# Routing attention and a feed-forward block on one core: a turn's products reordered by how they divide TensorE's array

## The chip, the core and the metric

One NeuronCore of a Trainium2 chip. The metric is the device time of one execution in microseconds, median of 3 runs. The engines are TensorE (PE, matrix products), VectorE (DVE), ScalarE (ACT), GpSimd (POOL) and SyncE (SP, which issues the DMAs here). Each engine takes its instructions in its own order, and waits on semaphores for the others.

TensorE's array has 128 x 128 cells. A product whose weights have fewer rows or columns than 128 uses a part of it, and two such products can stand in the array side by side. "How a product divides the array" means that choice: 128 x 128 (one product), 64 x 128 (two, by rows), 128 x 64 (two, by columns), 128 x 32 (four, by columns).

## The reference

Attention in which a query sees only the keys that are assigned to the same centroid, and then a feed-forward block with a quick GELU over the joined heads.

```
batch, n_heads, seq, head_dim = (4, 8, 768, 64)     # 16 clusters
q_assign = argmax(einsum('bhsd,hcd->bhsc', q_n, c_n))   # q_n, k_n, c_n: normalised
k_assign = argmax(einsum('bhsd,hcd->bhsc', k_n, c_n))
mask = q_assign[:, :, :, None] == k_assign[:, :, None, :]
scores = scale * matmul(q, k.transpose(0, 1, 3, 2))
scores = where(mask, scores, -1e9)
attn = exp(scores - max(scores)); attn /= sum(attn) + 1e-9
x = matmul(attn, v)  ->  (batch * seq, n_heads * head_dim) = (3072, 512)
h = x @ w_in                                         # 512 x 2048
g = h * (1 / (1 + exp(-1.702 * h)))
out = g @ w_out                                      # 2048 x 512
```

q, k, v and the centroids are fp32; the two weight matrices come in 8-byte floats and are turned into fp32 on the chip.

## The kernel before

`fast` does the work; `general`, a slower way for inputs outside a limit, is skipped here by a branch on a value that `fast` computes (`is_bad`).

**Units and turns.** Two heads make a pair, 16 pairs in all (`p`), each with its 768 positions on the free axis. A group is one pair and one half of its queries (384), and has six units, one per 128 keys. The main loop (L546) goes over turns `t`; a turn takes two units. Three turns make a group, 24 turns a batch (`TB`), 96 turns the whole, and two more end the pipeline. The first batch is special: its pairs (`p < HP`) are masked by adding a product on TensorE (`part`, L398) ahead of the exponential; the other pairs are masked afterwards, on DVE (`mask`, L420).

**What a turn does**, in the order in which it is written, which is the order of each engine's queue:

1. `scores` (L384): keys times queries of two heads, 64 x 128, into the PSUM pool `ps_s`, two buffers.
2. `part` (L398), first batch only.
3. `exps` (L409) on ACT.
4. `round_next`: one step of turning weights into fp32 (L159 to L177 on DVE, ACT and POOL), 33 steps in all; from turn 12 on there is a second one late in the turn.
5. `mask` (L420), four DVE instructions that read the exponentials in PSUM, and the running sum of the units on POOL (L430).
6. Half of the turn's feed-forward chunks.
7. `prep`, the preparation of a later pair, one step or more: `prep_turn` (four steps, transposes of q and k, L262, and their copy on ACT, L267), `prep_near` (centroid products L276, 128 x 32, and a copy L282), `prep_assign` (transposes L287, then argmax on DVE, L293 to L316), and `prep_hot` (first batch: L349, L354, L356) or `prep_spread` (L323, the copy L328 of a row of codes, and two DMAs, L330 and L332). Step 0 and steps 1 and 3 also issue the loads of v (L120), q and k (L111).
8. `values` of the turn before (L441): 128 x 64, into `ps_o`; after a group's last unit the copy L446.
9. Every third turn (t = 4, 7, 10, ...) `normalise` of a group: the sums over keys (L453, 128 x 64, with a matrix of ones), a reciprocal (L456) and a product (L458) on DVE, and on ACT two passes that accumulate the sums and the reciprocals for the branch's test (L462).
10. The other half of the feed-forward chunks.

**Feed-forward chunks.** When the four groups of half a batch are normalised, 28 chunks are put in the queue `ffn`: 16 of `first` (L480: four 128 x 128 products of 384 columns with w_in, tanh L485 on ACT, product L487 on DVE) and 12 of `second` (L497: four products of 512 columns with w_out; each fourth one ends with a copy L503 and a store L504). `rate` is 28 per 11.5 turns; `owed` carries the fraction.

**PSUM banks.** Transposes, centroid products, L323, L349, the sums of `normalise`, `first` and `second` all take their bank from the pool `ps_m`, whose three buffers are called `m`. A buffer is given again when its last reader is done, and a TensorE instruction that writes it waits for that reader. An accumulation of `second` holds its buffer for four chunks.

**The end.** After the loop DVE reduces the sums' test to one number by way of a transpose (L578 to L587); `values_load` (L589) makes every engine wait for it, and the chunks that are left, one half batch less one, follow.

Of the kernel before, what the change touches and what calls it, by code (L numbers as in the profile page):

```python
# [18 lines left out]
def kernel(  # L19
    tc: tile.TileContext,  # L20
    q: bass.AP,
    k: bass.AP,
    v: bass.AP,
    centroids: bass.AP,
    moe_w_in: bass.AP,
    moe_w_out: bass.AP,
    out: bass.AP,
):

    args = (q, k, v, centroids, moe_w_in, moe_w_out, out)
    bad = fast(tc, *args)
    with tc.If(bad > 0):
        general(tc, *args)
# [3 lines left out]
def fast(  # L39
# [33 lines left out]
    NF = DF // P  # L73
# [24 lines left out]
    def bank():  # L98
        return ps_m.tile([P, 512], FP32, name="m")

    def short():
        return tmp.tile([P, HALF], FP32, name="short")
# [4 lines left out]
    def load_qk(p, w):  # L107
        t = inp.tile([P, NJ, 2, D], FP32, name="in")
        b, hp = divmod(p, HP)
        for a in range(2):  # L110
            nc.sync.dma_start(  # L111
                out=t[:, :, a, :],
                in_=(q, k)[w][b, 2 * hp + a].rearrange("(p j) d -> p j d",
                                                       j=NJ))
        qk_in[p, w] = t

    def load_v(p):
        b, hp = divmod(p, HP)
        t = pairs.tile([P, 2, NJ, D], FP32, name="inv")
        nc.sync.dma_start(  # L120
            out=t.rearrange("p a j d -> p a (j d)"),
            in_=v[b, 2 * hp:2 * hp + 2].rearrange(
                "a (p j) d -> p a (j d)", j=NJ))
        v_in[p] = t
# [57 lines left out]
    def round_next():  # L182
        i = w_done[0]
        if i < NW:
            load_w(i + 2)
            split_w(i)
        if 0 < i <= NW:
            join_w(i - 1)
        w_done[0] += 1
# [66 lines left out]
    def prep_turn(p, i):  # L256
        w, h = divmod(i, 2)
        if h == 0:
            T[p, w] = pairs.tile([P, S], FP32, name=f"T{w}")
        ps = bank()  # L260
        for n in range(NH):
            nc.tensor.transpose(out=ps[:, n * P:(n + 1) * P],  # L262
                                in_=qk_in[p, w][:, h * NH + n].rearrange(
                                    "p a d -> p (a d)"),
                                identity=ident)
        dst = T[p, w][:, h * HALF:(h + 1) * HALF]
        nc.scalar.copy(dst, ps[:, 0:HALF])  # L267
# [95 lines left out]
    PREP = [lambda p, i=i: prep_turn(p, i) for i in range(4)]  # L363
# [9 lines left out]
    def split(g):  # L373
        b, r = divmod(g, 2 * HP)
        h, hp = divmod(r, HP)
        return b * HP + hp, h

    def scores(u):
        g, kt = divmod(u, NJ)
        p, h = split(g)  # L380
        ps = ps_s.tile([P, 2, 512], FP32, name="s")
        for a in range(2):
            rows = slice(a * D, (a + 1) * D)
            nc.tensor.matmul(out=ps[:, a, 0:HALF],  # L384
                             lhsT=T[p, 1][rows, kt * P:(kt + 1) * P],
                             rhs=T[p, 0][rows, h * HALF:(h + 1) * HALF],
                             start=True, stop=(p >= HP))
        s_of[u] = ps[:, :, 0:HALF]

    def part(u):  # L390

        g, kt = divmod(u, NJ)
        p, h = split(g)
        if p >= HP:
            return
        for a in range(2):
            r = 32 * (2 * (p % 2) + a)
            nc.tensor.matmul(  # L398
                out=s_of[u][:, a, :],
                lhsT=hots[p // 2, 1][r:r + NC, kt * P:(kt + 1) * P],  # L400
                rhs=hots[p // 2, 0][r:r + NC, h * HALF:(h + 1) * HALF],
                start=False, stop=True)

    def exps(u):
        p, h = split(u // NJ)
        s = s_of[u]
        if p < HP:
            A_of[u] = ap.tile([P, 2, HALF], FP32, name="A")
        nc.scalar.activation(out=A_of[u] if p < HP else s, in_=s, func=AF.Exp,  # L409
                             scale=SCALE)  # L410

    def mask(u):

        g, kt = divmod(u, NJ)
        p, h = split(g)
        s = s_of.pop(u)
        if p >= HP:
            A_of[u] = ap.tile([P, 2, HALF], FP32, name="A")
            for a in range(2):
                nc.vector.scalar_tensor_tensor(  # L420
                    out=A_of[u][:, a, :],
                    in0=qcode[p][:, a, h * HALF:(h + 1) * HALF],
                    scalar=code[p][:, kt % NH, 1, kt // NH, a:a + 1],
                    in1=s[:, a, :], op0=ALU.is_equal, op1=ALU.mult)
        A = A_of[u]
        if kt == 0:
            return
        if kt == 1:
            sum_of[g] = ap.tile([P, 2, HALF], FP32, name="sum", bufs=2)
        nc.gpsimd.tensor_tensor(out=sum_of[g],  # L430
                                in0=A_of[u - 1] if kt == 1 else sum_of[g],
                                in1=A, op=ALU.add)

    def values(u):
        g, kt = divmod(u, NJ)
        p, h = split(g)
        if kt == 0:
            o_of[g] = ps_o.tile([P, 512], FP32, name="o")
        A = A_of.pop(u)
        for a in range(2):  # L440
            nc.tensor.matmul(out=o_of[g][a * D:(a + 1) * D, 0:HALF],  # L441
                             lhsT=v_in[p][:, a, kt, :], rhs=A[:, a, :],
                             start=(kt == 0), stop=(kt == NJ - 1))
        if kt == NJ - 1:
            O_of[g] = xp.tile([P, HALF], FP32, name="x")
            nc.scalar.copy(O_of[g], o_of.pop(g)[:, 0:HALF])  # L446

    def normalise(g):

        sm = sum_of.pop(g)  # L450
        ps = bank()
        for a in range(2):
            nc.tensor.matmul(out=ps[a * D:(a + 1) * D, 0:HALF], lhsT=ones,  # L453
                             rhs=sm[:, a, :], start=True, stop=True)
        rec = short()
        nc.vector.reciprocal(out=rec, in_=ps[:, 0:HALF])  # L456
        x = xT_of[g] = O_of.pop(g)
        nc.vector.tensor_tensor(out=x, in0=x, in1=rec, op=ALU.mult)  # L458

        junk = short()  # L460
        for i, t in enumerate((ps[:, 0:HALF], rec)):
            nc.scalar.activation(out=junk, in_=t, func=AF.Copy,  # L462
                                 accum_out=sums[:, i, g:g + 1])
        if g % HP == HP - 1:
            ffn.extend(ffn_chunks(g // HP))


    ffn = deque()
# [50 lines left out]
    prep_at = {}  # L519
    for p in range(1, NPAIR):  # L520
        b, hp = divmod(p, HP)
        for i in range(2 if p == 1 else 0, len(PREP)):
            if p == 1:
                t = (i - 2) // 2
            elif b == 0:
                t = (hp - 2) * TG + 1 + i // 2
            else:
                t = b * TB + (-20, -8, -2, 1)[hp] + i
# [5 lines left out]
    def prep(p, i):  # L534
        if i == 0 and p:
            load_v(p)
        PREP[i](p)
        if i in (1, 3) and loads:
            load_qk(*loads.popleft())

    rate = (NF + NH * (NF // 4)) / (TB / 2 - 0.5)
    owed = 0.0
# [3 lines left out]
    for t in range(NT + 2):  # L546
        us = range(2 * t, 2 * t + 2) if t < NT else ()
        for u in us:
            scores(u)
        if t == 0:  # L550
            prep(0, 6)
        for u in us:
            part(u)
        for u in us:
            exps(u)
        round_next()
        for u in us:
            mask(u)
        owed = owed + rate if ffn else 0.0
        n = min(int(owed), len(ffn))  # L560
        owed -= n
        for _ in range((n + 1) // 2):
            ffn.popleft()()
        for p, i in prep_at.get(t, ()):
            prep(p, i)
        if 1 <= t <= NT:
            for u in range(2 * t - 2, 2 * t):
                values(u)
        if t >= 2 and (t - 2) % TG == TG - 1:
            normalise((t - 2) // TG)  # L570
        if t >= TB // 2:
            round_next()
        for _ in range(n // 2):
            ffn.popleft()()


    ok = const.tile([P, 2, 2 * NPAIR], FP32, name="ok")
# [1 line left out]
                            op0=ALU.is_le)  # L579
    ok1 = const.tile([P, 1], FP32, name="ok1")  # L580
    nc.vector.tensor_reduce(out=ok1, in_=ok, axis=AX.XY, op=ALU.min)
    ps = bank()
    nc.tensor.transpose(out=ps[0:1, 0:P], in_=ok1, identity=ident)
    okt = const.tile([1, 1], FP32, name="okt")
# [448 lines left out]
```

## Time and profile before

| | us |
|---|---|
| median of 3 runs (1107.4, 1107.4, 1109.77) | 1107.4 |
| the profiled execution | 1111.25 |
| its span, first to last instruction | 1109.4 |
| L480, busy (1024 records, two per product) | 359.1 |
| L497, busy (768) | 348.7 |
| L384, busy (768) | 151.9 |
| L441, busy (768) | 149.8 |
| L262, busy (192) | 32.9 |
| L456 on DVE, mean of one | 2.557 |
| L462 on ACT, mean of one, from PSUM | 0.492 |

An fp32 product shows as two records of TensorE. The record's duration reaches beyond the start of the next one, since products are pipelined; what a product costs is read from start to start. In the timeline rows of one form that follow one another are merged ("x8"), with the start of the first, the time from there to the end of the last, engine, line, operation, tiles, shapes; in brackets stands how long the engine was idle before and what ended that.

Turn starts can be read from the first L384 of each turn: turn 14 at 103.13, turn 24 (the first of the second batch) at 222.73, turn 37 at 372.73, turn 38 at 376.31, turn 40 at 393.63, turn 41 at 405.67, turn 42 at 414.49, turn 95, the last with scores, at 986.33.

### The profile page before, as it was taken

The page shows a single profiled execution, that of the slowest core. Times are in us where ns is not written, and L with a number is a line of the kernel's source. Part 1 is how long each engine was busy: PE and PEld are TensorE (multiplying, and loading weights), DVE is VectorE, ACT ScalarE, POOL GpSimd, SP SyncE. Part 2 cuts the span into 40 slices and gives each one's busy share as a digit, 9 for nine tenths or more (in the row PEclk, how much of TensorE's full clock was granted, in tenths as well). Part 3 has the DMA queues.
Part 4 walks back from the last instruction along what each step waited for, and adds up shares of the span by engine and source line. Part 5 has one row for each costly group of instructions (what it writes and reads, how often), then busy time and mean ns, then how long its engine had stood idle before and what let it go on. Part 6 is the DMA issues. An engine that isn't in the chain of part 4 may idle for free. (4 is left out here: it accounts for less than half of the span.)

```text
span 1109.4 us, 10492 instructions
## 1 busy us (share of the span) xinstructions
PE 1069.4 (96%) x3982; PEld 490.4 (44%) x3982; DVE 470.0 (42%) x711; ACT 348.3 (31%) x665; POOL 338.6 (31%) x200
## 2 busy tenths in 40 slices
PE   6786999999999999999999999999999999999997
PEld 3332454444443445444444445444544444444543
DVE  4779986134542444323543254433452244421200
ACT  4564554233322333223331233223322132211100
POOL 2577655322222333122231243223132233320000
PEclk9989899999999999999999999999999999999999
DMA  9443342110100010101100000020000000000000
GB/s 232 135 130 105 116 128 71 46 48 20 45 22 27 10 29 15 31 25 53 50 22 17 19 15 16 14 67 12 8 8 10 9 10 1 1 10 19 1 10 22
DMA packets 64812, 45.13 MB, mean 41 GB/s; under 512 B 51952, under 2 KB 57584, under 8 KB 64752
## 3 DMA queue, kind: packets, MB, share of 16 engines
q1 hardware_dynamic: 64608, 44.33, 14.2%
q8 instruction: 33, 0.54, 0.2%
q14 instruction: 27, 0.22, 0.1%
q10 hardware_dynamic: 144, 0.03, 0.0%
HBM read 38.04 MB, written 6.31 MB: 40 GB/s over the span
## 5 line engine op out<-in xcount | busy, mean ns | idle before, releaser
L480 PE MATMUL m<-x,w_in 128*128 128x384 f32 x1024 | 359.1, 499 | 6.2 <-DVE x L458 4.8
L430 POOL TENSOR_TENSOR sum<-sum,A 128x768 f32<-128x768 f32 x128 | 234.1, 1829 | 382.8 <-DVE A L420 366.6
L497 PE MATMUL m<-w_out,g 128*128 128x512 f32 x768 | 348.7, 601 | 0.0
L480 PEld LDWEIGHTS m<-x,w_in 128*128 128x128 f32 x1024 | 188.0, 191 | 171.2 <-issue 40.6
L420 DVE SCALAR_TENSOR_TENSOR A<-qb,code,s 128x384 f32<-128x384 uint8 x288 | 157.6, 610 | 250.3 <-ACT s L409 226.7
L497 PEld LDWEIGHTS m<-w_out,g 128*128 128x128 f32 x768 | 140.2, 190 | 188.8 <-issue 185.0
L487 DVE SCALAR_TENSOR_TENSOR g<-g,m 128x384 f32<-128x384 f32 x128 | 70.9, 554 | 200.5 <-ACT g L485 199.7
L384 PE MATMUL s<-T,T 64*128 64x384 f32 x768 | 151.9, 514 | 2.6 <-ACT A L409 2.6
L441 PE MATMUL o<-A,inv 128*64 128x384 f32 x768 | 149.8, 512 | 0.0
L409 ACT ACTIVATE s<-s 128x768 f32<-128x768 f32 x144 | 107.9, 791 | 94.0 <-PE s L384 93.8
L485 ACT ACTIVATE g<-m 128x384 f32<-128x384 f32 x128 | 62.4, 487 | 217.1 <-PE m L480 217.0
L456 DVE RECIPROCAL short<-m 128x384 f32<-128x384 f32 x32 | 81.8, 2557 | 103.7 <-PE m L453 103.7
L430 POOL TENSOR_TENSOR sum<-A 128x768 f32<-128x768 f32 x32 | 58.9, 1842 | 190.7 <-DVE A L420 190.5
L384 PEld LDWEIGHTS s<-T,T 64*128 64x128 f32 x768 | 66.5, 188 | 90.5 <-issue 50.0
L441 PEld LDWEIGHTS o<-A,inv 128*64 128x64 f32 x768 | 47.5, 139 | 69.7 <-issue 68.5
L462 ACT ACTIVATE short<-m 128x384 f32<-128x384 f32 x32 | 15.7, 492 | 142.9 <-DVE short L456 142.9
L503 ACT ACTIVATE y<-m 128x512 f32<-128x512 f32 x24 | 14.3, 594 | 102.4 <-PE m L497 89.0
L267 ACT COPY T<-m 128x384 f32<-128x384 f32 x64 | 29.5, 479 | 46.8 <-PE m L262 46.7
L409 ACT ACTIVATE A<-s 128x768 f32<-128x768 f32 x48 | 36.2, 809 | 23.7 <-PE s L398 23.7
L446 ACT COPY x<-o 128x384 f32<-128x384 f32 x32 | 15.4, 480 | 77.0 <-PE o L441 77.0
L177 POOL TENSOR_TENSOR w_in<-w_in,e 128x512 f32<-128x512 f32 x16 | 24.7, 1543 | 44.6 <-DVE w_in L174 42.2
L262 PE MATMUL m<-ident,in 128*128 128x128 f32 x192 | 32.9, 291 | 4.1 <-ACT qb L356 1.7
(67 smaller groups left out, 397.9 us busy)
## 6 DMA issues: line engine op xcount, KB each, us to landing
raw<-in_moe_w_in_dram SPq DMA_DIRECT2D x16, 512.0 KB, 4.6
raw<-in_moe_w_out_dram SPq DMA_DIRECT2D x16, 512.0 KB, 3.5
in<-in_q_dram SPq DMA_DIRECT2D x32, 192.0 KB, 3.7
in<-in_k_dram SPq DMA_DIRECT2D x32, 192.0 KB, 3.5
inv<-in_v_dram SPq DMA_DIRECT2D x16, 384.0 KB, 4.5
out_dram<-y SPq DMA_DIRECT2D x24, 256.0 KB, 2.0
qb<-line SPq DMA_DIRECT2D x12, 192.0 KB, 3.0
line<-row SPq DMA_DIRECT2D x12, 1.5 KB
```

What stands on the lines that cost most here:

```text
L262: nc.tensor.transpose(out=ps[:, n * P:(n + 1) * P], in_=qk_in[p, w][:, h * NH + n].rearrange("p a d -> p (a d)"), identity=ident)
L267: nc.scalar.copy(dst, ps[:, 0:HALF])
L384: nc.tensor.matmul(out=ps[:, a, 0:HALF], lhsT=T[p, 1][rows, kt * P:(kt + 1) * P], rhs=T[p, 0][rows, h * HALF:(h + 1) * HALF], start=True, ...
L409: nc.scalar.activation(out=A_of[u] if p < HP else s, in_=s, func=AF.Exp, scale=SCALE)
L420: nc.vector.scalar_tensor_tensor(out=A_of[u][:, a, :], in0=qcode[p][:, a, h * HALF:(h + 1) * HALF], scalar=code[p][:, kt % NH, 1, kt // NH ...
L430: nc.gpsimd.tensor_tensor(out=sum_of[g], in0=A_of[u - 1] if kt == 1 else sum_of[g], in1=A, op=ALU.add)
L441: nc.tensor.matmul(out=o_of[g][a * D:(a + 1) * D, 0:HALF], lhsT=v_in[p][:, a, kt, :], rhs=A[:, a, :], start=(kt == 0), stop=(kt == NJ - 1))
L456: nc.vector.reciprocal(out=rec, in_=ps[:, 0:HALF])
L480: nc.tensor.matmul(out=ps[:, 0:HALF], lhsT=w_in[:, c, f * P:(f + 1) * P], rhs=xT[c], start=(c == 0), stop=(c == NCH - 1))
L485: nc.scalar.activation(out=g, in_=ps[:, 0:HALF], func=AF.Tanh, scale=0.851)
L487: nc.vector.scalar_tensor_tensor(out=g, in0=g, scalar=1.0, in1=ps[:, 0:HALF], op0=ALU.add, op1=ALU.mult)
L497: nc.tensor.matmul(out=ps[:, 0:DM], lhsT=hs[f][:, n * P:(n + 1) * P], rhs=w_out[:, f, :], start=(f == 0), stop=(f == NF - 1))
```

## The change

The order within a turn becomes: scores, part, exponentials, `round_next`, mask; then of the preparation only the centroid products (`prep_near`); then values of the turn before; then `normalise`, where there is one; then the other steps of the preparation; then the second `round_next`; then all feed-forward chunks of the turn in one piece. `prep` is called in a different order but with the same steps in each turn, so its DMAs go along with it. The chunks are popped one at a time while `owed` is 1 or more. At the end, eight `first` chunks are issued ahead of the transpose of the branch's test. Nothing is added or left out.

```diff
         for u in us:
             mask(u)
-        owed = owed + rate if ffn else 0.0
-        n = min(int(owed), len(ffn))
-        owed -= n
-        for _ in range((n + 1) // 2):
-            ffn.popleft()()
-        for p, i in prep_at.get(t, ()):
-            prep(p, i)
+        work = sorted(prep_at.get(t, ()), key=lambda w: PREP[w[1]] != prep_near)
+        while work and PREP[work[0][1]] == prep_near:
+            prep(*work.pop(0))
         if 1 <= t <= NT:
             for u in range(2 * t - 2, 2 * t):
                 values(u)
+        owed = owed + rate if ffn else 0.0
         if t >= 2 and (t - 2) % TG == TG - 1:
             normalise((t - 2) // TG)
+        for p, i in work:
+            prep(p, i)
         if t >= TB // 2:
             round_next()
-        for _ in range(n // 2):
+        while owed >= 1 and ffn:
             ffn.popleft()()
+            owed -= 1
...
     nc.vector.tensor_reduce(out=ok1, in_=ok, axis=AX.XY, op=ALU.min)
+    for _ in range(NF // 2):
+        ffn.popleft()()
     ps = bank()
     nc.tensor.transpose(out=ps[0:1, 0:P], in_=ok1, identity=ident)
```

## The prediction

> **What bounds the kernel now.** First the page: the busy shares, the slices, the clock.
>
> ```profile
> PE 1069.4 (96%) x3982; PEld 490.4 (44%) x3982; DVE 470.0 (42%) x711; ACT 348.3 (31%) x665; POOL 338.6 (31%) x200
> ...
> PE   6786999999999999999999999999999999999997
> ...
> PEclk9989899999999999999999999999999999999999
> ```
>
> TensorE (PE) is idle for some 31 us of the first 120 (table of stretches: 18.5, 22.5, 26.7 and 21.0 busy of 30 each) and then hardly at all until the end (199.9 of 200 from 400 to 600); DVE is next at 42%. From 120 us on every ns of PE's row counts, so I read it in the timeline, here turns 40 to 42. "x8" are eight records, two per fp32 product; start to start is the price.
>
> ```profile
> 400.81 1.51 PE L441 MATMUL o<-A,inv 128*64 128x384 f32 x8
> ...
> 402.15 0.82 PE L453 MATMUL m<-sum,ones 128*64 128x384 f32 x4
> ...
> 402.89 2.85 PE L480 MATMUL m<-x,w_in 128*128 128x384 f32 x8
> ...
> 405.61 0.49 ACT L462 ACTIVATE short<-m 128x384 f32<-128x384 f32 x1 [4.16 <-DVE short L456]
> ...
> 405.67 1.56 PE L384 MATMUL s<-T,T 64*128 64x384 f32 x8
> ...
> 407.16 2.85 PE L480 MATMUL m<-x,w_in 128*128 128x384 f32 x8
> ...
> 409.85 0.49 PE L262 MATMUL m<-ident,in 128*128 128x128 f32 x3
> ...
> 410.27 1.51 PE L441 MATMUL o<-A,inv 128*64 128x384 f32 x8
> ```
>
> At the end, where L480 runs without interruption, chunks follow every 2.58 us:
>
> ```profile
> 1025.94 0.49 ACT L485 ACTIVATE g<-m 128x384 f32<-128x384 f32 x1 [2.09 <-PE m L480]
> ...
> 1028.52 0.49 ACT L485 ACTIVATE g<-m 128x384 f32<-128x384 f32 x1 [2.09 <-PE m L480]
> ```
>
> So a record takes 2.58/8 = 0.323. Between other shapes the chunk takes 405.67 - 402.89 = 2.78, 0.20 more. L384 is four pairs, 1.29, and takes 407.16 - 405.67 = 1.49, again 0.20 more. L441 takes 1.34 when L453, its own shape, follows (0.05 over 1.29), and 1.44 when L480 does (411.71 - 410.27, next row). Three transposes take 0.42 before L441, 0.33 among themselves (0.109 each). A change of shape thus costs **0.10 on leaving**, and **on entering** 0.10 for L480, L497 and L384, 0.05 for L441, 0.06 for transposes (L276 to L262 to L441: 252.37 to 252.85 is 0.48, not 0.42).
>
> **The change: what it removes.** In the order of the built program a turn with feed-forward work has four changes before (L384, block, L441, block, L384) and three after. Counted from turn 14 to the end there are 373 before and 281 after: 92 leavings, 92 x 0.10 = 9.2 us. Entries by L480 or L497 fall from 161 to 37 (124 x 0.10 = 12.4), entries by transposes rise from 13 to 45 (32 x 0.06 = 1.9), those of L384, L441 and L276 stay equal in number. **Gain 19.7, say 20 us.** Transposes directly ahead of L480 or L497, 45 times, are not in this trace: nothing if the next weights load under 0.109 as they do among transposes, 0.10 each (4.5 in all) if as badly as across a change; I take nothing, the nearer row.
>
> **What it moves: normalise, ahead of transposes and feed-forward.** Its L453 takes one of the three "m" banks. The bank comes free when L462 has read it, and L462 waits for the reciprocal L456 (4.16 above). Before, behind L453 came one feed-forward block with two banks free. Now the transposes (up to two banks), L323 (one) and the whole block come behind it, and in the built program's waits a PE instruction of 18 of those turns waits for that L462. The wait, with its price, occurs once in the early part before:
>
> ```profile
> 50.09 2.56 DVE L456 RECIPROCAL short<-m 128x384 f32<-128x384 f32 x1 [4.96 <-PE m L453]
> ...
> 52.74 0.49 ACT L462 ACTIVATE short<-m 128x384 f32<-128x384 f32 x1 [4.27 <-DVE short L456]
> ...
> 53.38 0.55 PE L262 MATMUL m<-ident,in 128*128 128x128 f32 x3 [0.61 <-ACT short L462]
> ```
>
> When is the bank free? Count from the start S of the turn's scores. The reciprocal stands behind the turn's four masks on DVE. Turn 37, which has no feed-forward, already has the new order:
>
> ```profile
> 372.73 1.56 PE L384 MATMUL s<-T,T 64*128 64x384 f32 x8
> ...
> 374.64 2.19 DVE L420 SCALAR_TENSOR_TENSOR A<-qb,code,s 128x384 f32<-128x384 uint8 x4 [11.44 <-ACT s L409]
> ...
> 376.75 2.55 DVE L456 RECIPROCAL short<-m 128x384 f32<-128x384 f32 x1
> ```
>
> The reciprocal starts at S + 4.02, L462 2.58 later (its row there is 379.33), PE goes on 0.64 after that (52.74 to 53.38): **S + 7.24**. When does PE want it? Scores 1.49, values 1.34, sums 0.74: S + 3.57. L323 takes 0.15 (343.04 to 343.19), three transposes 0.33 + 0.06, a chunk 2.58. By the order of each turn:
> - L323, then transposes without a bank (turns 46, 70): wanted at 3.72, 3.52 each, 7.0. Turn 22 has no masks (reciprocal 0.86 after L453, as 402.15 to 403.01) but 0.43 of L398: 3.2.
> - Two groups of transposes (25, 49, 73): the second at 3.96, 3.28 each, 9.8.
> - L323 and two groups (28, 52): 4.11, 3.13; then 0.5 for the copy L328, queued on ACT behind both L462 (1.23, 405.61 to 406.84) and taking 0.25; 7.3.
> - L323, transposes, chunk (31, 55, 76): 4.11, 3.13 each, 9.4.
> - One of the two, then two chunks (40, 43, 64, 67; 79; 16, 19): the second chunk at 6.54, 6.4 and 6.97: 4 x 0.70 + 0.84 + 2 x 0.38 = 4.4.
>
> **Loss 41 us**, eleven waits of over 3 us (36.7) and seven short ones. The other turns have a bank. Below bound of this term: nothing, if the bank came free by S + 3.7; above: 18 x 3.65 = 66, if every one waited in full.
>
> Queued behind L462 on ACT are now the copies of transposes (L267) and the tanh (L485), ahead of it before: used a turn later, or when their chunk ends, so free. L330 and L332 are issued some 4 us later on SP; their first reader is at least two turns (18 us) on, against 3.0 to land. The loads L111 and L120 that go along with prep on SP are read three turns on or later, against 3.7 to 4.5 to land. The sums that L453 reads, now up to 6 us sooner, are done by POOL a turn before (two L430 of 1.85 behind masks). Values come up to 6 us earlier, at S + 1.49, a whole turn after the masks that end at S + 4.1 of the turn before: free; if a turn shrank to 3.58, as turn 37, still 0.97 left.
>
> **What the waits do to the clock.** The table of stretches (PE busy of 3.41 us, then DVE, ACT, POOL, the clock):
>
> ```profile
> 36.15:39.56 3.41, 1.19 (x11) 0.65 (x9) 1.68 (x3) 2.34 (x5) 2.18 (x3) 1.00 0.31 72
> 39.56:42.98 3.42, 3.42 (x13) 1.34 (x10) 3.28 (x8) 0.48 (x1) 0.95 (x1) 0.50 0.21 81
> ...
> 56.63:60.04 3.41, 1.50 (x14) 0.34 (x12) 0.89 (x2) 3.41 (x8) 3.41 (x2) 1.00 1.04 262
> ...
> 97.59:101.00 3.41, 1.83 (x12) 0.49 (x8) 2.66 (x2) 0.72 (x1) 3.33 (x3) 1.00 0.52 163
> 101.00:104.42 3.42, 2.16 (x12) 0.80 (x12) 3.42 (x3) 2.03 (x3) 3.42 (x3) 1.00 0.00 0
> ```
>
> The clock changes on a grid of 3.41 us. Stretches with PE busy 1.50 or less (five) are followed by half speed, of 3.4, 6.8, 3.4, 6.8 and 3.4 us; those with 1.81 or more are not. A wait of 3.1 to 3.5 leaves under 1.75 busy in one stretch wherever it starts, but for about one start in ten. Half speed costs 1.7 per stretch, two stretches where the idle time runs on past the edge by 0.5 or more (about a third of the starts). I take 2.0 for each of eleven: **22 us**; ends 0 and 11 x 3.41 = 37.5.
>
> The Trainium skill, "TensorE: Matmul & The Clock Gate", section on HAM oscillation, says that only idle gaps above about 3.4 us should be avoided, a whole window. By it most of these waits would leave the clock alone and the sum would be 1124 as in the first rival; the trace shows half speed after 1.9 us of idle time in a stretch, and I go by the trace.
>
> **Before turn 14** PE waits for ACT and DVE. Values now stand where PE waited for L282 (2.95, 2.22, 2.46; 1.5 hidden each), for L308 (0.8), for L316 (2.0), for x at the first chunk (1.5 of 4.83): -8.8. In turns 4 and 7 transposes now wait for L462: 7.35 - 4.86 = 2.5 each, of which turn 4 waited 1.7 already: +3.3. DVE, 27.9 busy of 30 from 90 to 120, gives some back: **-4**, between -9 and +5. **At the end** the test waits behind the last early chunk's tanh and product on DVE instead of 0.93 for L581: 0, within 1.
>
> Sum: -20 + 41 + 22 - 4 = **+39** on the span of 1109.4, so 1148. That execution took 1111.25, 3.85 above the median of 1107.4; the difference carries over: **1146**.
>
> **The rivals.**
> - *The clock holds.* Waits as above, no half speed: 1107.4 + 17 = 1124. For it: short waits in 97 to 104 us passed. Against: five of five deep stretches did not. 0.17.
> - *Two stretches after each wait*: 1107.4 - 20 + 41 + 37 - 4 = 1161. For it: two of five. 0.10.
> - *Faster: normalise's bank isn't late.* If L462 read it without the reciprocal, or the reciprocal passed the masks, eleven waits would vanish: 1107.4 - 24 = 1083. It decides from a release before S + 5.7, where the long waits are halved and stay under the clock's 1.9. Against: L462 waits for L456 in all rows seen, and DVE keeps its order. 0.05; break-even near that point 0.02.
>
> **How the numbers follow.** 0.66 for the sum, 1146. Its own terms reach from 1134 to 1160. The range takes the clock's rival in: 1120 to 1162. A change under 0.3% (3.3 us) can't be told from none; only the last rival gets there. Faster 0.05, same 0.02, slower 0.93.
>
> **What would show it.** Among PE's waits after the change, L262, L480 and L497 for ACT L462: about 18 from turn 14 on, some 40 us, the longest 3.5; 0.5 in the clock right behind them; L441 1.49 behind L384; chunks of 2.58 from the second on. Wrong if PE stays at 99.9% from 200 to 1000 us, or if the clock keeps 1.00 through waits of 3 us.

## The result, and the profile after

| | before | after |
|---|---|---|
| median, the two run side by side (4 runs each) | 1108.45 us | 1147.78 us |
| lowest to highest | 1107.4 to 1109.77 | 1145.69 to 1150.5 |
| profiled span | 1109.4 | 1145.4 |
| mean granted TensorE clock | 0.989 | 0.976 |

The ratio is **1.0356, 95% interval 1.0329 to 1.0382**: the change makes the kernel 3.6% slower. The page of the changed kernel, busy shares, slices and clock:

```profile
PE 1066.3 (93%) x3982; PEld 500.1 (44%) x3982; DVE 486.7 (42%) x711; ACT 350.3 (31%) x665; POOL 336.3 (29%) x200
...
PE   6787799988989999898889999988989999999997
...
PEclk9899999999999999999999999999999999999999
```

TensorE does the same 3982 instructions in 3 us less busy time, but its slices, which before read 9 without a break from the fifth to the last but one, now have 8s in three groups. Each group lies at the start of a batch of 24 turns, where the turns with normalise whose preparation also wants banks stand close together (turns 22 to 31, 46 to 55, 70 to 76). What PE waited for there, from 118 us to the end (total us, times, longest):

```profile
PE m L262 <- ACT short L462: 25.3, 8, 3.4
PE m L480 <- ACT short L462: 14.4, 10, 3.0
PE m L480 <- DVE g L487: 3.1, 1, 3.1
...
PE m L480 <- ACT row L328: 0.5, 2, 0.2
```

That is 39.7 us in 18 waits for L462, the pass that reads normalise's bank; before, no PE wait of that kind was left after 118 us. One of them in full, in the timeline of turn 28 of the changed kernel:

```profile
275.17 1.56 PE L384 MATMUL s<-T,T 64*128 64x384 f32 x8
...
276.66 1.51 PE L441 MATMUL o<-A,inv 128*64 128x384 f32 x8
...
277.09 2.19 DVE L420 SCALAR_TENSOR_TENSOR A<-qb,code,s 128x384 f32<-128x384 uint8 x4 [0.74 <-ACT s L409]
...
278.00 0.82 PE L453 MATMUL m<-sum,ones 128*64 128x384 f32 x4
...
278.90 0.55 PE L262 MATMUL m<-ident,in 128*128 128x128 f32 x3
279.19 2.55 DVE L456 RECIPROCAL short<-m 128x384 f32<-128x384 f32 x1
281.78 0.49 ACT L462 ACTIVATE short<-m 128x384 f32<-128x384 f32 x1 [4.10 <-DVE short L456]
...
282.42 0.55 PE L262 MATMUL m<-ident,in 128*128 128x128 f32 x3 [2.97 <-ACT short L462]
...
283.21 7.12 PE L480 MATMUL m<-x,w_in 128*128 128x384 f32 x16 [0.25 <-ACT row L328]
```

Read it from the bottom up. PE's second group of transposes waits 2.97 for the bank of L453. ACT sat idle for 4.10 before L462, the bank's last reader: its first pass needs only the sums, but it starts at 281.78, 0.04 after the reciprocal L456 ended on DVE. L456 reads the same bank, so that the bank has two readers that come late. DVE starts the reciprocal when the turn's four masks end. The 16 records of L480 behind it span 7.12, though two chunks span 5.33 at full speed. The table of stretches says why (PE busy is the second number, the granted clock the third from the right):

```profile
276.92:280.34 3.42, 2.53 (x16) 0.97 (x12) 3.25 (x5) 0.76 (x2) 1.89 (x2) 1.00 0.00 0
280.34:283.75 3.41, 1.09 (x5) 0.72 (x6) 2.10 (x2) 1.94 (x7) 1.72 (x1) 1.00 0.00 0
283.75:287.16 3.41, 3.41 (x7) 1.79 (x6) 0.00 (x0) 0.15 (x1) 0.00 (x0) 0.50 0.21 64
...
829.88:833.30 3.42, 2.14 (x14) 0.83 (x10) 3.42 (x5) 0.37 (x1) 2.27 (x2) 1.00 0.00 0
833.30:836.71 3.41, 1.72 (x6) 1.06 (x7) 1.71 (x2) 1.71 (x6) 1.33 (x1) 1.00 0.00 0
836.71:840.12 3.41, 3.41 (x12) 1.90 (x10) 0.56 (x1) 0.49 (x1) 0.00 (x0) 1.00 0.16 58
```

After the stretch in which PE was busy for 1.09, the clock is 0.50 for one stretch: 3.41 us at half speed, 1.71 lost. The last three rows are turn 76, whose wait is as long (2.97 too) but is divided by the grid's edge into 1.28 and 1.69 of idle time: the clock stays at 1.00, and that turn is 2.84 us longer than before, where turns 31 and 55, with the same order of work, are 4.29 and 4.45 longer.

### The profile page after: what moved, and what is told of

Same layout as the page of the kernel before. It is cut to its first block, busy times and chain, and to the rows that moved or that the text cites. A ratio compares the mean times of both kernels' runs of the same rounds, so it can differ in the third digit from the quotient of the medians.

```text
span 1145.4 us, 10477 instructions
## 1 busy us (share of the span) xinstructions
PE 1066.3 (93%) x3982; PEld 500.1 (44%) x3982; DVE 486.7 (42%) x711; ACT 350.3 (31%) x665; POOL 336.3 (29%) x200
## 5 line engine op out<-in xcount | busy, mean ns | idle before, releaser
L480 PE MATMUL m<-x,w_in 128*128 128x384 f32 x1024 | 352.6, 499 | 22.3 <-ACT short L462 14.4
L497 PE MATMUL m<-w_out,g 128*128 128x512 f32 x768 | 345.8, 606 | 0.0
L480 PEld LDWEIGHTS m<-x,w_in 128*128 128x128 f32 x1024 | 193.7, 194 | 166.8 <-ACT short L462 19.4
L497 PEld LDWEIGHTS m<-w_out,g 128*128 128x128 f32 x768 | 146.8, 195 | 179.6 <-issue 177.3
L487 DVE SCALAR_TENSOR_TENSOR g<-g,m 128x384 f32<-128x384 f32 x128 | 70.4, 553 | 269.7 <-ACT g L485 269.4
L384 PE MATMUL s<-T,T 64*128 64x384 f32 x768 | 154.2, 521 | 5.4 <-ACT A L409 5.4
L441 PE MATMUL o<-A,inv 128*64 128x384 f32 x768 | 145.6, 500 | 0.0
L456 DVE RECIPROCAL short<-m 128x384 f32<-128x384 f32 x32 | 81.7, 2552 | 27.2 <-PE m L453 27.2
L441 PEld LDWEIGHTS o<-A,inv 128*64 128x64 f32 x768 | 46.8, 136 | 84.6 <-issue 84.6
L262 PE MATMUL m<-ident,in 128*128 128x128 f32 x192 | 37.2, 317 | 35.2 <-ACT short L462 32.3
L462 ACT ACTIVATE short<-m 128x384 f32<-128x384 f32 x32 | 15.7, 491 | 127.6 <-DVE short L456 127.6
L262 PEld LDWEIGHTS m<-ident,in 128*128 128x128 f32 x192 | 23.2, 155 | 55.3 <-ACT short L462 34.2
L171 DVE SCALAR_TENSOR_TENSOR e<-raw,e 128x512 int32<-128x512 int32 x32 | 33.7, 1054 | 2.7 <-ACT e L163 2.7
```

The lines of the kernel that those rows point to most:

```text
L171: nc.vector.scalar_tensor_tensor(out=e, in0=raw[:, :, 1], scalar=-2 ** 31, in1=e, op0=ALU.bitwise_and, op1=ALU.bitwise_or)
L262: nc.tensor.transpose(out=ps[:, n * P:(n + 1) * P], in_=qk_in[p, w][:, h * NH + n].rearrange("p a d -> p (a d)"), identity=ident)
L384: nc.tensor.matmul(out=ps[:, a, 0:HALF], lhsT=T[p, 1][rows, kt * P:(kt + 1) * P], rhs=T[p, 0][rows, h * HALF:(h + 1) * HALF], start=True, ...
L441: nc.tensor.matmul(out=o_of[g][a * D:(a + 1) * D, 0:HALF], lhsT=v_in[p][:, a, kt, :], rhs=A[:, a, :], start=(kt == 0), stop=(kt == NJ - 1))
L480: nc.tensor.matmul(out=ps[:, 0:HALF], lhsT=w_in[:, c, f * P:(f + 1) * P], rhs=xT[c], start=(c == 0), stop=(c == NCH - 1))
L487: nc.vector.scalar_tensor_tensor(out=g, in0=g, scalar=1.0, in1=ps[:, 0:HALF], op0=ALU.add, op1=ALU.mult)
```

## The experiments

All ratios are to the kernel before, run side by side with the experiment on the same chip. The theory: the loss comes from one bank, which normalise's L453 fills and which is held until the reciprocal and then L462 have read it, and from the half-speed clock behind the waits for it; the saving of shape changes is real and lies under it. The rivals: the new order as such costs (a longer block of chunks, values sooner), or the copies of the transposes, queued on ACT behind L462, are what is late.

**Prep alone (e5).** The kernel before, with only the preparation moved behind values and normalise; chunks stay in two pieces.

```diff
-        for p, i in prep_at.get(t, ()):
-            prep(p, i)
         if 1 <= t <= NT:
             for u in range(2 * t - 2, 2 * t):
                 values(u)
         if t >= 2 and (t - 2) % TG == TG - 1:
             normalise((t - 2) // TG)
+        for p, i in prep_at.get(t, ()):
+            prep(p, i)
```

> The kernel before, with one part of the change alone: the preparation is called behind values and normalise; feed-forward stays in two halves, 360 changes of shape instead of 373 (3.8 us less). Bank theory: eleven turns have two or three steps behind the sums that need the third bank, 2.8 to 3.3 us each, 32 us, and half speed after eight to ten of them, 14 to 17 us: 1107.4 - 4 + 32 + 15 + 2 = 1152, between 1143 and 1160. Rival (one block of feed-forward is what costs): 1104.

Measured 1142.96 us, ratio 1.0306 (1.027 to 1.0341). This one move, which saves hardly any shape changes (360 are left of 373), loses 34 us by itself. PE's waits from 130 us on:

```profile
PE m L262 <- ACT short L462: 13.7, 5, 2.8
PE m L497 <- ACT short L462: 8.0, 3, 2.7
PE m L480 <- ACT short L462: 7.9, 3, 2.6
```

They are 29.6 us in eleven. The time is 9 under the middle of what was expected, at its very edge (1143). Some 5 of that is the clock, since only six of the eleven waits are followed by half speed, where eight to ten were expected, and some 2 the waits, expected at 32; the rest wasn't traced. These waits are 2.6 to 2.8, the ones of the changed kernel 3.0 to 3.4. Four rows of the table of stretches of this run:

```profile
516.38:519.79 3.41, 1.49 (x6) 0.96 (x7) 1.80 (x2) 1.94 (x6) 0.00 (x0) 1.00 0.74 196
519.79:523.20 3.41, 3.41 (x12) 1.45 (x12) 0.00 (x0) 0.63 (x2) 0.00 (x0) 1.00 0.09 34
...
553.92:557.34 3.42, 1.38 (x6) 0.88 (x7) 1.68 (x2) 2.08 (x7) 0.00 (x0) 1.00 0.00 0
557.34:560.75 3.41, 3.41 (x7) 1.50 (x5) 0.00 (x0) 0.00 (x0) 0.00 (x0) 0.50 0.34 92
```

Busy for 1.49, and the clock holds; busy for 1.38, and it halves.

**The bank set free early (e1, e2).** The changed kernel, with L462's first pass, the one that reads PSUM, ahead of the reciprocal. It leaves a copy in SBUF, from which the reciprocal is taken: the same sums, but the bank no longer waits for DVE. The edit takes both late readers off the bank, the pass and the reciprocal; neither was moved alone.

```diff
-        rec = short()
-        nc.vector.reciprocal(out=rec, in_=ps[:, 0:HALF])
+        cp = short()
+        nc.scalar.activation(out=cp, in_=ps[:, 0:HALF], func=AF.Copy,
+                             accum_out=sums[:, 0, g:g + 1])
+        rec = short()
+        nc.vector.reciprocal(out=rec, in_=cp)
         x = xT_of[g] = O_of.pop(g)
         nc.vector.tensor_tensor(out=x, in0=x, in1=rec, op=ALU.mult)
-        junk = short()
-        for i, t in enumerate((ps[:, 0:HALF], rec)):
-            nc.scalar.activation(out=junk, in_=t, func=AF.Copy,
-                                 accum_out=sums[:, i, g:g + 1])
+        nc.scalar.activation(out=cp, in_=rec, func=AF.Copy,
+                             accum_out=sums[:, 1, g:g + 1])
```

> The changed kernel, but L462's first pass reads the sums ahead of the reciprocal and leaves a copy in SBUF, which the reciprocal reads; its second pass stays where it was. Theory (normalise's PSUM bank is late, because its reader waits for the reciprocal): the bank is free at about S + 4.3 instead of 7.25, so of the 18 waits A, B and D shrink to 0.2 to 0.6 each; the row copy L328 still stands behind the second pass, which waits for the reciprocal, so turns 28 and 52 keep 2.8 and turns 31, 55, 76 keep 0.6. Sum 11 us of waits and some 3 of clock: 1107.4 - 20 - 4 + 14 = 1097. Rival (the queue of ACT, which still holds the copies and the tanh behind a pass that waits for the reciprocal): no change against the changed kernel, 1147. Rival (feed-forward in one piece costs by itself): above 1130.

Measured 1104.11 us, ratio 0.9949 (0.9934 to 0.9964): 45 us gone from the changed kernel by an edit that leaves the order of PE's work alone. It is 7 above what was expected. The kernel before, run beside it, took 1109.71, 2.3 more than the 1107.4 of the sum; the rest wasn't traced, and it isn't in the waits, of which there are no more than foreseen. From 130 us on they are, but for 0.3 and the one at the end:

```profile
PE m L480 <- ACT row L328: 7.3, 5, 2.8
PE m L262 <- ACT short L456: 2.2, 6, 0.5
```

(L456 is the first pass here.) The second pass still waits for the reciprocal, and behind it on ACT stands the copy of the row of codes, L328, whose bank is late in its place: 2.8 in turns 28 and 52, 0.5 in turns 31, 55 and 76, as the theory expected. So the second rival, the queue of ACT, is true of these 7.3 us of waits and one stretch of half speed behind them (from 272.81), not of the whole loss. e2 also moves the second pass, behind the turn's chunks:

```diff
-        nc.scalar.activation(out=cp, in_=rec, func=AF.Copy,
-                             accum_out=sums[:, 1, g:g + 1])
+        late.append(lambda: nc.scalar.activation(
+            out=cp, in_=rec, func=AF.Copy, accum_out=sums[:, 1, g:g + 1]))
...
         while owed >= 1 and ffn:
             ffn.popleft()()
             owed -= 1
+        while late:
+            late.pop()()
```

> As the run before, and L462's second pass is issued behind the turn's feed-forward chunks. Bank theory: waits of 3.7 us in all are left (262 wanting the bank 0.2 to 0.6 before S + 4.3), no half speed between 130 and 1000 us; the 20 us of the order come out whole: 1107.4 - 20 - 4 + 4 = 1087. If the price of a change of shape were mis-sized, the time is above 1095.

Measured 1092.0 us, ratio 0.984 (0.9812 to 0.9867), 5 above what was expected, with the kernel before 2.3 above the sum's 1107.4 as for e1. From 130 us to the end of the loop PE waits for little more than this, and the clock never leaves 1.00 from 130 to 1000 us:

```profile
PE m L262 <- ACT short L458: 2.2, 6, 0.5
```

So the order asked for by the change is 1.6% quicker than the one before, when normalise's bank is read at once and the second pass is out of the copies' way.

**Normalise last (e3, run again as e13).** The other way to take the bank out of the others' path: normalise as it was, but behind the turn's chunks (in the last turn at its old place, since nothing follows).

```diff
-        if t >= 2 and (t - 2) % TG == TG - 1:
+        last = t == NT + 1
+        if last:
             normalise((t - 2) // TG)
...
             owed -= 1
+        if t >= 2 and (t - 2) % TG == TG - 1 and not last:
+            normalise((t - 2) // TG)
```

> The changed kernel with normalise as it was before, but called behind the turn's feed-forward chunks, except in the last turn. 305 changes of shape from turn 14 on instead of 281, 3.6 us more; no product of the turn takes a bank behind the sums. Bank theory: no waits for L462 after turn 14, 1107.4 - 20 + 4 - 5 = 1086. Rival (the loss comes from values first, or from one block of feed-forward): near 1147, since both are kept.

Measured 1090.23 us, ratio 0.9824 (0.9796 to 0.9851), 4 above what was expected. L462 is gone from PE's waits after 130 us, although its own wait for the reciprocal is untouched: what follows it on PE is the next turn's scores and values, which take no `m` bank. This is all that the table has left, the branch's test at the end:

```profile
PE m L480 <- DVE bad L592: 2.0, 1, 2.0
```

e3 keeps values first and the chunks in one piece, so neither of them is the loss. It has 24 shape changes more than e2 (305 to 281) and isn't slower; e2 still has its 2.2 us of waits, and by the prices the 24 should cost 3.6. Run again beside e11 and e12:

> e3 once more, on the same chip as the two others, to rank them: 0.982 of before, 1090.

Measured 1091.2 us, ratio 0.9843 (0.9827 to 0.9859).

**Preparation last (e8).** The changed kernel with the remaining steps of prep behind the chunks; normalise stays, so chunks follow it at once and find banks free.

```diff
-        for p, i in work:
-            prep(p, i)
...
             owed -= 1
+        for p, i in work:
+            prep(p, i)
```

> The changed kernel with normalise untouched and in its place, but the preparation (all but the centroid products) called behind the feed-forward chunks. The third bank is then asked for at S + 8.9 or later, the bank of the sums is free at S + 7.25: no waits of over 1 us for L462 after turn 14. 289 changes of shape, 3.0 us more than the changed kernel by their prices: 1108 - 17 - 4 = 1087. If the wait had to do with normalise ahead of feed-forward as such, it would be near 1147.

Measured 1096.24 us, ratio 0.9895 (0.9873 to 0.9917), 9 above what was expected. The wait for L462 is down to 0.4 us, as the theory says, but a new one takes its place: transposes right behind the chunks want banks that the chunks have just used.

```profile
PE m L262 <- DVE g L487: 4.1, 6, 1.8
```

Of the 9, some 5 lie before turn 17, which starts at 142.43 in the trace instead of 141.41 where 4 less was expected (the wait of 1.8 is in them); the other 4 are the five later waits of 0.47 each and one stretch of half speed, 1.7.

**Controls (e6, e7).** e2's edit put into the kernel before, where there was next to no wait for L462 to remove (one of 0.6 us):

> The kernel before, with its order, and normalise as in e2 (L462's first pass ahead of the reciprocal, the second behind the turn's last chunk). A control: in the old order PE hardly waited for that bank, so theory expects no change, 1108, within 3 us. If freeing the bank were a gain of its own, 1095 or less, and e2 would owe its time to that and not to the order.

Measured 1111.05 us, ratio 1.0041 (1.0027 to 1.0055). The edit itself gains nothing; here it is 0.4% dearer. And e2's edit put into e5, so that e7 and e2 differ in the order alone, the eight chunks at the end included:

> e5 with the same normalise as e2. Bank theory: the 32 us of waits and the half speed behind them go, some 3 us of short waits stay, and 3.8 us of changes of shape are saved: 1108 - 4 + 3 - 2 = 1105, against 1143 of e5. Against e2 (281 changes of shape, this has 360: 15.8 us by the prices read in the trace of before) it measures the price of dividing the block: 1092 + 15 = 1107. Rival (the price of a change of shape is below 0.1): within 8 us of e2.

Measured 1108.0 us, ratio 0.9996 (0.9983 to 1.001). e7 has 79 more shape changes than e2 (360 to 281) and no waits to speak of (0.6 us for that bank from 130 us on); the difference of the ratios, 0.0156, is 17 us, or 0.22 for one change. The traces agree where nothing but the loop counts: from turn 17 to turn 95 e7 takes 844.56 and e2 829.14, of which 1.3 and 2.2 are waits, and e7 has 75 changes more there, 0.21 to 0.22 each. That is the price of a shape change with the waits for the bank out of the way.

**Sums next to values (e11, e12, e14).** L453 has the shape of L441, so normalise directly ahead of values saves the same changes and gives the bank 1.3 us more. e11 is e2 with normalise there:

```diff
+        if t >= 2 and (t - 2) % TG == TG - 1:
+            normalise((t - 2) // TG)
         if 1 <= t <= NT:
             for u in range(2 * t - 2, 2 * t):
                 values(u)
         owed = owed + rate if ffn else 0.0
-        if t >= 2 and (t - 2) % TG == TG - 1:
-            normalise((t - 2) // TG)
```

> e2 with normalise ahead of values, which have its shape: the sums start at S + 1.49 instead of 2.83 and their bank is free at about S + 3.1, before the 3.7 at which the transposes want it. The 2.2 us of waits that e2 still has for the first pass (six, 0.2 to 0.5) go: 1092 - 2 = 1090. If those waits were not the bank's, no change.

Measured 1103.12 us, ratio 0.9955 (0.9941 to 0.997): 13 above what was expected, a miss. `m<-x,w_in` (L482 here) now waits 15.4 us for x, the product on DVE (L463), 7.3 of them in one wait, before turn 14. e12 puts normalise back to its old place in the first half batch (t up to 13) and moves two first chunks ahead of the point where all engines wait for the test:

```diff
+        if 2 <= t <= TG * HP + 1 and (t - 2) % TG == TG - 1:
+            normalise((t - 2) // TG)
         if t >= TB // 2:
             round_next()
...
+    for _ in range(2):
+        ffn.popleft()()
     is_bad = nc.values_load(bad[0:1, 0:1], min_val=0, max_val=1)
```

> e11, but in the first half batch normalise stays behind the preparation (there transposes wait for the copy L354, which stands behind the reciprocal on DVE: 4.3 us in two waits), and two more first chunks are issued between the transpose of the branch's test and the load of its result (2.0 us, and 1.7 of half speed). 1090 - 4 - 3 = 1083, between 1080 and 1090.

Measured 1091.98 us, ratio 0.9857 (0.984 to 0.9874), 9 above what was expected: the first wait is gone, but at the start of six of the seven later half batches one is left:

```profile
PE m L482 <- DVE x L463: 7.6, 6, 1.7
```

The queue `ffn` is filled inside normalise. Where normalise stands ahead of the line that adds `rate` to `owed`, the first chunks of the new half batch are taken in the same turn, before DVE has made their x. e14 moves that one line ahead of normalise, as it stands in the changed kernel, so that they are taken a turn later wherever the queue had run empty (turns 37, 61 and 85):

```diff
+        owed = owed + rate if ffn else 0.0
         if t >= 2 and t > TG * HP + 1 and (t - 2) % TG == TG - 1:
             normalise((t - 2) // TG)
         if 1 <= t <= NT:
             for u in range(2 * t - 2, 2 * t):
                 values(u)
-        owed = owed + rate if ffn else 0.0
```

> The same computation as e12 (the sums' passes free their bank early, normalise ahead of values from the second half batch on, prep last), with one line moved: the chunks of a new half batch are owed only after the early normalise has been issued, so that they start one turn later, as in the changed kernel. Theory: the waits of e12 for x (7.6 us in 6 waits from 130 us on) come from chunks that are taken in the very turn that issues normalise, and go; 1092.0 - 7.6 = 1084 us, a ratio of about 0.979, between 1081 and 1089. Rival: x is late for another reason, the waits stay, 1092 us, a ratio of 0.986. If it is under e3 (0.982 to 0.984) by more than its interval, it is the quickest order that was tried.

Measured **1081.55 us, ratio 0.9751 (0.9729 to 0.9773)**, the quickest order that was tried: 2.5% under the kernel before and 5.8% under the changed one (0.9751/1.0356 = 0.942). Between 130 and 1075 us its table of PE's waits is empty, and its slices are full again:

```profile
PE 1048.6 (97%) x3982; PEld 492.7 (46%) x3982; DVE 481.0 (45%) x711; ACT 346.0 (32%) x665; POOL 338.1 (31%) x200
...
PE   7886999999999999999999999999999999999997
```

**The end (e9).** e3 with the two first chunks ahead of that same point.

> e3, and at the end two more first chunks between the transpose of the branch's test and the load of its result, which every engine waits for. The 2.0 us for L592's result and the half speed of 3.4 us behind it (1.7) lie under 5.2 us of products: 1090.2 - 3.7 = 1086.5. Rival (the load itself holds PE): no change, 1090.

Measured 1088.39 us, ratio 0.9832 (0.9814 to 0.985), not to be told from e3's 0.9824. The part from turn 95 on is 2.2 us shorter in the trace (118.66 against 120.86) and the wait for L592 is gone, but the part before turn 17 is 1 longer; whether the edit gains is open.

## Why the prediction was right

The forecast was 1146, the measured time 1147.78; the mechanism, the place and four of the five terms came out. That the forecast is within 2 us is in part luck, as the sum below shows. Term by term, from the trace of the changed kernel against the one before:

- **Shape changes, -20.** From turn 17 on, turns without normalise are shorter by 0.19 to 0.24 each, turns 29 and 53 by 0.40, turns 38, 62 and 86 by 0.53; turns 26, 50 and 74 hand a chunk to the turn ahead of them and say nothing. The whole follows from the starts of turns 17 and 95: the changed kernel is 0.9 ahead at the first and 36.5 behind at the second, +37.4; of that 37.2 are waits for L462, 0.5 for L328 and 17.1 half speed, which leaves -17.4 for the order. Idle time counts each wait some 0.15 too short (see the next term), 2.6 for the 17 waits in this part, and by that estimate the order itself gains the 20 foreseen. Transposes directly ahead of L480, which the trace before did not show and which the prediction took at nothing extra, do cost nothing: from the last L262 to L480 or L497 is 0.109, as among transposes.
- **Waits for the bank, +41.** Measured 39.7 in 18. The bank was foreseen free at S + 7.24; in turn 28 PE goes on at 282.42, S + 7.25. The eleven long waits are 34.2 and the two for L328 0.5, against 36.7 foreseen; each is some 0.15 shorter, since the profile counts idle time from the modelled end of the record before. The seven short ones are 5.5 against 4.4: turn 16 alone waits 2.49 where 0.38 was foreseen. e1, e2 and e3 show the cause: with the bank free early, or taken last, the waits go.
- **Clock, +22.** This is the term that was mis-sized: 17. Ten of the eleven waits are followed by half speed, and all ten by one stretch. The step that failed is "two stretches where the idle time runs on past the edge by 0.5 or more (about a third of the starts)": in turns 46 and 70 it runs on by 0.67 and 0.51, and one stretch is all that follows. The traces show part of what the step lacked: how much of the half-speed stretch itself PE works. In the traces of all 14 kernels, each of the 14 half-speed stretches with PE busy for 2.59 or less was followed by a second one, as here in the kernel before:

  ```profile
  111.24:114.66 3.42, 2.53 (x6) 1.03 (x8) 3.42 (x4) 1.62 (x5) 2.43 (x2) 0.50 0.05 18
  ```

  With PE busy for 2.75 to 3.36 in it, 3 of 17 were, among them the other double one of the kernel before (60.04 to 63.46, 2.87); turns 46 and 70 have 2.75 and 2.90 and were not:

  ```profile
  754.79:758.20 3.41, 2.90 (x6) 1.71 (x7) 0.57 (x1) 1.70 (x6) 0.16 (x1) 0.50 0.00 0
  ```

  Of 78 that PE filled, four were all the same. So 0.5 us of idle time past the edge wasn't enough here, and 0.8 was each time; what decides between, and the four, stay open.
- **Before turn 14, -4.** The changed kernel starts turn 14 earlier by 2.97 and turn 17 by 0.9; in between, turn 14 is shorter by 5.05 (PE waited 5.6 in it before), and turns 15 and 16 lose 4.2 to waits for DVE's product L487, which the prediction didn't have. With turn 16's 2.49, which is counted above, taken out, it is -3.4 at turn 17.
- **The end, 0.** From turn 95 on the difference changes by -0.5: the test's waits were 0.93 and 1.24, and are 1.96 in one place.

Together -17.4 + 37.2 + 0.5 + 17.1 - 0.9 - 0.5 = +36.0 on the span, against +39. Two misses nearly cancel, which is luck: the sum was 3 high, and the 3.85 us by which the profiled execution stood above its median, which the prediction let carry over, were not there after the change; so 39.3 between the medians.

Of the rivals, "the clock holds" fell at the first long wait, and "two stretches" with all ten. "Normalise's bank isn't late" fell for the change as it was made, but e1 and e2 make its condition true, the pass without the reciprocal, and get 1104 and 1092, where the rival's sum was 1083. The condition as the prediction words it was one step short: the reciprocal reads the bank too, so it had to be given the copy.

What isn't settled: e14 is quicker than e12 by 8.8 us of span, although it starts turn 17 1.8 later; of the 10.6 that it gains from there on, 8.0 are e12's waits (7.6 of them for x), and the remainder wasn't traced. Three chunks of `second` also go from the loop to the end, which moves their time and doesn't save it.

## What to carry to other kernels

A PSUM bank of a rotating pool is held until its last reader is done, so a pass over it that comes only after a slow result of another engine holds the bank for all of that time, here until S + 7.24: let the engine that needn't wait read first, and leave a copy in SBUF for the slow one. When work is reordered for one resource (here the array's shape), count for each moved instruction what the instructions behind it want, banks above all, because work that takes no bank is what hid the release before. A wait of 3 us on the engine that sets the time costs nearly 5 when the clock halves behind it (2.97 and 1.71 in turn 28).

## What the runs showed of the hardware

**The clock's border.** Over four runs (the changed kernel, e1, e5 and e8), from 118 us to 1075, all 17 stretches of 3.41 us with PE busy 1.40 or less were followed by half speed. Of ten between 1.43 and 1.63, four were and six were not; above that none was. In the early parts single ones with more were: 1.76 in e1, 1.94 in e6, 1.96 in e9. So the border in the loop is not a whole idle stretch but some 1.8 to 2.0 us of idle time in one, early on 1.5 to 1.7 in three cases, and whether a wait of 2.6 to 3 us costs 1.7 more depends on where it falls on the grid. The Trainium skill, "TensorE: Matmul & The Clock Gate", Part 1, gives the window as 3413 ns and free-running, which these rows show too (the half-speed stretches of the changed kernel, from 17.51 to 1079.06, start whole multiples of 3.413 apart); its section on HAM oscillation puts the limit at idle gaps above about 3.4 us, and there the measurement differs: four of five waits of 2.97 halve the clock.

**A shape change** costs about 0.2 us for these fp32 products (17 us for 79 in e7 against e2). The Trainium skill, "TensorEngine Tiling (Array Packing)", Key Properties, says that a change of tiling mode drains TensorE, without a price; these runs give one.
